# A two-layer transformer prompt kernel: three reciprocals of softmax sums moved to GpSimd as a power, the last tile's columns and store rearranged, and a new order list

## The chip, the cores and the metric

The kernel runs on one core of a Trainium2 chip. The core has five engines that run side by side, each with its own list of instructions: TensorE (PE, matmuls; PEld is its weight load), VectorE (DVE), ScalarE (ACT), GpSimd (POOL) and SyncE (SP, which only issues transfers). They wait for each other through semaphores. The metric is the device time of one execution in microseconds, as the median of several runs.

## What is computed

Two layers, each made twice with the same weights, on x of 2048 rows and 512 columns in bf16: attention over a sliding block of 256 keys with 32 heads of 16 columns, and an MLP of 1792 columns with gelu. Cut to what matters:

```python
def _A_ref(x, wqkv, wo):            # H = 32; Dh = 16; W = 256
    qkv = (x @ wqkv).reshape(B, S, 3, H, Dh)...
    scores = einsum("bhqd,bhkd->bhqk", q, k) * Dh ** -0.5
    mask = (i - j >= 0) & (i - j < W)
    p = softmax(where(mask, scores, -1e9))
    o = einsum("bhqk,bhkd->bhqd", p, v)
    return o.reshape(B, S, D) @ wo

def _B_ref(x, w1, b1, w2, b2):      # F = 1792
    return gelu(x @ w1 + b1) @ w2 + b2

x = x + _A_ref(layernorm(x)); x = x + _B_ref(layernorm(x))
x = x + _A_ref(layernorm(x)); x = x + _B_ref(layernorm(x))
```

## The kernel before

x lies in SBUF as 16 tiles of 128 rows; with the two repetitions there are 32 tile visits, called tau 0 to 31. Attention works on blocks b of two tiles (16 blocks), the MLP on jobs of two or four tiles.

For each block, Q, K and V are projected on TensorE into PSUM and copied out: Q and V by VectorE or ScalarE (line 725 or 727, whichever the list says), K by VectorE (line 853). The scores of a block are made in visits of 512 columns times four row groups, with small matmuls that run four at a time (`QT,KT`); ScalarE takes the exponential of each half visit (`E<-ps`, line 965), and VectorE or GpSimd multiplies the parts on the block's edge by a 0/1 mask (line 981).

P times V (`E,Va`) is made in pairs of 128-column groups, two pairs a block, so 32 in the whole kernel. V carries a column of ones, so each head's softmax sum comes out beside its 16 columns. Of each pair VectorE transposes the result out of PSUM into TT (line 1031); then the reciprocal of the sums is written into a spare column of TT, called Rc (line 1034, 32 numbers a partition); then TM = TT times Rc (line 1036, on VectorE or GpSimd); then VectorE transposes TM into OT (line 1041). There is one TT buffer and there are two TM buffers. When both pairs of a block are done, TensorE multiplies OT by `Wo_sb`, VectorE adds the result to x (line 793), and the layernorm for the MLP follows: statistics on VectorE (740, 742), the power -0.5 of the variance on GpSimd (744, one number a partition, with the constant tile `mhalf`), the scaling on VectorE or GpSimd (747), and a transposition by a trip through DRAM (two DMAs on SyncE's queue) or on TensorE. GpSimd adds b2 to x (1075).

The MLP multiplies by W1 (`xnTB,W_sb`), takes the gelu on ScalarE, either straight from PSUM (line 1111) or in wide pieces after VectorE has added b1 (lines 1100 and 1103), and multiplies by W2 (`W_sb,gT`). The exponential and the gelu need different tables on ScalarE; a change of table is a load of its own (ACT_TABLE_LOAD). The result is added to x (793), and in the second repetition each tile is stored from SyncE's queue as soon as it is done (1126). The very last tile, tau 31, is done in two column groups (1138, 1140), so that its addition and store can begin before its last matmul.

The program is recorded as some 3,200 nodes, each with an engine, what it reads and writes, and sometimes an alternative on another engine. Three tables of numbers, written out in the source, say the rest: `ORDER` the order in which the nodes are taken (each engine then runs its own in that order), `TURNS` which alternative each node with a choice takes, and `BANKS` which of the eight PSUM banks each group gets. The durations in the calls of `add` serve only to place waits within TensorE's stream; they do not change the order, which is given. GpSimd nodes that the source holds to be long (over 600 in any alternative) also wait for the VectorE operation marked `lock` that stands before them in the list.

Of the kernel before, what the change touches and what calls it, by code (L numbers as in the profile page):

```python
# [6 lines left out]
dt = mybir.dt  # L7
ALU = mybir.AluOpType
# [295 lines left out]
def bass_interleave_layers__sliding_block__dense_activation_gelu__prompt_kernel(  # L304
# [11 lines left out]
    Bb, S, D = A_x.shape  # L316
    assert Bb == 1
    P = 128
    T = S // P
    DC = D // P  # L320
    Dh = 16
# [63 lines left out]
    with ExitStack() as kctx:  # L385
        S_ = _Sched(nc, kctx)

        def sb(name, shape, dtype=dt.bfloat16):
            return kctx.enter_context(nc.sbuf_tensor(name, shape, dtype))
# [8 lines left out]
        statmv = sb("statmv", [P, NST, 2], dt.float32)  # L398
        mhalf = sb("mhalf", [P, 1], dt.float32)
# [15 lines left out]
        TT = sb("TT", [P, NTT, 2, 2, 8, 32], dt.float32)  # L415
        hot = TT[:, 0, 0, 0, 0, 0:HC]
        Rc = TT[:, :, :, :, :, VW]
# [211 lines left out]
        add = PL.add  # L629
# [5 lines left out]
            reads=["ident"], writes=["ident"])  # L635
# [573 lines left out]
```

## Time and profile before

| | us |
|---|---|
| median of 3 runs | 437.96 |
| lowest, highest | 437.73, 438.31 |
| the profiled execution | 437.65 |
| its span, first to last instruction | 435.8 |

The granted TensorE clock is 1.00 throughout. Some of the costliest groups (line, engine, operation, shapes, how many, then busy us and mean ns of one, then the idle time of the engine before them):

```profile
L965 ACT ACTIVATE E<-ps 128x1024 bf16<-128x1024 f32 x300 | 283.9, 1039 | 21.5 <-PE ps L32 20.0
L793 DVE TENSOR_TENSOR X<-X,ps 128x512 bf16<-128x512 bf16 x63 | 42.4, 679 | 25.7 <-PE ps L32 25.2
L1031 DVE STREAM_TRANSPOSE TT<-ps 128x1024 f32<-128x1024 f32 x32 | 39.9, 1247 | 11.8 <-PE ps L32 11.3
L740 DVE BATCH_NORM_STATS2 stat<-X 128x6 f32<-128x512 bf16 x64 | 42.6, 675 | 0.5 <-DMA X<-in_A_x_dram 0.2
```

How to read it: an engine's busy time says how much it has to do, and the idle time before a group says what it waited for. The chain of waits follows the work that ended last back to the start, at each step to whatever released it; time on that chain is time that the span consists of. Matmuls are pipelined, so one matmul's duration is longer than the step to the next one.

### The profile page before, as it was taken

Reading aid. Unit: us, or ns where it says so; the run is one execution under the profiler, and the core shown is the slowest. Engines: PE = TensorE matmul, PEld = TensorE weight load, DVE = VectorE, ACT = ScalarE, POOL = GpSimd, SP = SyncE. Lnnn points to the kernel's source line nnn. Section 1 sums busy time; section 2 is a strip of 40 time slices with the busy share of each in tenths; the row PEclk is TensorE's granted clock in tenths of the full one; section 3 lists DMA queues with packets and bytes.
Section 4 is the critical chain, followed back from the end, with each engine's and each line's share of the span. In section 5 each row is a group of like instructions: output and inputs, shape, how many; then the busy total and the mean of one; then the engine's idle time right before and its main releaser. Section 6 shows DMA issues by size and latency. Waiting matters only on the chain.

```text
span 435.8 us, 18376 instructions
## 1 busy us (share of the span) xinstructions
PE 419.3 (96%) x8281; PEld 251.6 (58%) x8338; DVE 367.3 (84%) x753; ACT 389.1 (89%) x452; POOL 272.4 (63%) x294
## 2 busy tenths in 40 slices
PE   8999999999799999999999999999999999999997
PEld 5767757665555546565555655644566554454674
DVE  6999999999999888999889788988989894766712
ACT  5999999999989999899898999799899999899551
POOL 6797949848755857858386556984535465576120
DMA  8930000001211023012211013000231003002201
GB/s 263 372 107 5 3 3 3 2 5 50 77 39 39 14 64 75 15 38 74 52 27 43 21 50 87 6 2 26 75 107 32 15 8 92 2 3 63 87 2 48
DMA packets 39898, 22.81 MB, mean 52 GB/s; under 512 B 24588, under 2 KB 39308, under 8 KB 39820
## 3 DMA queue, kind: packets, MB, share of 16 engines
q1 hardware_dynamic: 39404, 21.24, 16.7%
q8 instruction: 65, 1.06, 1.0%
q10 hardware_dynamic: 416, 0.39, 0.3%
q14 instruction: 13, 0.11, 0.1%
HBM read 13.77 MB, written 7.86 MB: 50 GB/s over the span
## 4 chain that ended last, share of the span: by engine, by line
PE 81%; ACT 14%; DVE 2%; issue 1%; DMA 1%; POOL 0%
PE ps L32 80%; ACT E L965 10%; ACT gT L1103 2%; ACT L1103 1%; PE ps L36 1%; ACT gT L1111 1%; ACT L965 1%; DMA X<-in_A_x_dram 1%; DVE stat L740 0%; DVE TT L1031 0%; DVE X L793 0%; DVE E L981 0%; DVE xn L747 0%; POOL statmv L744 0%; DVE X L1138 0%
## 5 line engine op out<-in xcount | busy, mean ns | idle before, releaser
L965 ACT ACTIVATE E<-ps 128x1024 bf16<-128x1024 f32 x300 | 283.9, 1039 | 21.5 <-PE ps L32 20.0
L981 POOL TENSOR_TENSOR E<-E,mask 128x512 bf16<-128x512 bf16 (+1 forms) x131 | 140.9, 1091 | 75.0 <-DVE E L981 39.7
L32 PE MATMUL ps<-xnTB,W_sb 128*128 128x512 bf16 (+1 forms) x560 | 117.3, 337 | 0.6 <-DVE E L981 0.2
L32 PE MATMUL ps<-W_sb,gT 128*128 128x512 bf16 (+2 forms) x419 | 107.7, 373 | 3.2 <-issue 2.4
L32 PE MATMUL ps<-xnTA,Wqkv_sb 128*128 128x256 bf16 (+1 forms) x544 | 74.2, 267 | 1.4 <-ACT E L965 1.1
L32 PEld LDWEIGHTS ps<-xnTB,W_sb 128*128 128x128 bf16 x560 | 51.8, 98 | 36.8 <-DVE TT L1031 0.2
L793 DVE TENSOR_TENSOR X<-X,ps 128x512 bf16<-128x512 bf16 x63 | 42.4, 679 | 25.7 <-PE ps L32 25.2
L32 PE MATMUL ps<-QT,KT 32*128 32x64 bf16 (+3 forms) x2392 | 60.6, 217 | 3.2 <-ACT E L965 1.2
L32 PEld LDWEIGHTS ps<-W_sb,gT 128*128 128x128 bf16 x462 | 40.1, 98 | 37.7 <-ACT gT L1111 0.5
L32 PEld LDWEIGHTS ps<-QT,KT 32*128 32x128 bf16 x2392 | 34.5, 92 | 46.9 <-ACT E L965 28.1
L32 PEld LDWEIGHTS ps<-xnTA,Wqkv_sb 128*128 128x128 bf16 x544 | 47.9, 98 | 17.4 <-ACT E L965 2.5
L981 DVE TENSOR_TENSOR E<-E,mask 128x512 bf16<-128x512 bf16 (+1 forms) x125 | 48.5, 415 | 9.8 <-ACT E L965 9.4
L1031 DVE STREAM_TRANSPOSE TT<-ps 128x1024 f32<-128x1024 f32 x32 | 39.9, 1247 | 11.8 <-PE ps L32 11.3
L1100 DVE TENSOR_SCALAR gT<-ps,b1T 128x512 bf16<-128x512 f32 (+1 forms) x72 | 45.0, 649 | 4.7 <-PE ps L32 4.2
L744 POOL TENSOR_TENSOR statmv<-statmv,mhalf 128x1 f32<-128x1 f32 x64 | 36.4, 577 | 18.7 <-DVE statmv L742 18.5
L32 PE MATMUL ps<-E,Va 64*17 64x64 bf16 (+3 forms) x3904 | 46.1, 229 | 2.0 <-PE ps L32 0.8
L1075 POOL TENSOR_TENSOR X<-X,b2b 128x512 bf16<-128x512 bf16 x32 | 36.9, 1154 | 16.9 <-DVE TM L1036 8.8
L1111 ACT ACTIVATE gT<-ps,b1T 128x512 bf16<-128x512 f32 (+1 forms) x68 | 36.0, 586 | 12.6 <-PE ps L32 12.4
L32 PEld LDWEIGHTS ps<-E,Va 64*17 64x17 bf16 x3904 | 36.8, 85 | 15.7 <-PE ps L32 5.1
L1036 POOL TENSOR_TENSOR TM<-TT 128x512 bf16<-128x512 f32 x24 | 26.6, 1107 | 27.0 <-DVE E L981 15.9
L853 DVE TENSOR_TENSOR KT<-ps,parmask 128x512 bf16<-128x512 f32 (+1 forms) x68 | 41.0, 644 | 2.4 <-PE ps L32 2.2
L740 DVE BATCH_NORM_STATS2 stat<-X 128x6 f32<-128x512 bf16 x64 | 42.6, 675 | 0.5 <-DMA X<-in_A_x_dram 0.2
(57 smaller groups left out, 380.3 us busy)
## 6 DMA issues: line engine op xcount, KB each, us to landing
scr_x<-xs_ SPq DMA_DIRECT2D x44, 128.0 KB, 1.8
W_sb<-in_B_w_dram SPq DMA_DIRECT2D x2, 1792.0 KB, 15.4
xnTB<-scr_x SPq DMA_DIRECT2D x26, 128.0 KB, 2.6
xnTA<-scr_x SPq DMA_DIRECT2D x18, 128.0 KB, 2.4
out_dram<-X SPq DMA_DIRECT2D x15, 128.0 KB, 1.9
Wqkv_sb<-in_A_wqkv_dram SPq DMA_DIRECT2D x4, 256.0 KB, 4.9
X<-in_A_x_dram SPq DMA_DIRECT2D x1, 1024.0 KB, 10.0
Wqkv_sb<-in_A_wqkv_dram SPq DMA_DIRECT2D x1, 512.0 KB, 6.3
```

Source lines behind the costliest of these rows:

```text
L32: return self.e.matmul(*a, **k)
L740: add("dve", lambda e, B: e.bn_stats(stat6[:, k6, 0:6], X[:, t, :]), 598, reads=["X%d" % t], writes=["st%d" % k6], prio=prio)
L744: add("pool", lambda e, B: e.tensor_tensor(out=statmv[:, m, 1:2], in0=statmv[:, m, 1:2], in1=mhalf[:], op=ALU.pow), 535, reads=["mv%d" % m ...
L793: add("dve", lambda e, B: e.tensor_tensor(out=X[:, t, :], in0=X[:, t, :], in1=ps[:, B[g][0], :], op=ALU.add), d_psum(512), reads=["X%d" % ...
L853: x = e.tensor_tensor(out=dst.rearrange("p (g s) (a k) -> p s g a k", s=2, a=2)[:, s], in0=src.rearrange("p (g s k) -> p s g k", s=2, k=HK ...
L965: add("act", lambda e, B, g_=g_, gi=gi: e.activation(E[:, 2 * gi : 2 * gi + 2, e0 : e0 + 512], ps[:, B[g_][0] : B[g_][0] + 2, :], AF.Exp, ...
L981: op = lambda e, B, Ew=Ew, Mw=Mw: e.tensor_tensor(out=Ew, in0=Ew, in1=Mw, op=ALU.mult)
L1031: add("dve", lambda e, B: e.transpose(TT[:, s].rearrange("p a c q d -> p a (c q d)"), ps[:, B[g][0] : B[g][0] + 2, :].rearrange("p a n -> ...
L1036: mul = lambda e, B: e.tensor_tensor(out=TM[:, sm].rearrange("p c q a d -> p a (c q) d"), in0=TT[:, s, :, :, :, 0:Dh].rearrange("p a c q d ...
L1075: add("pool", lambda e, B: e.tensor_tensor(out=X[:, t, :], in0=X[:, t, :], in1=b2b[:], op=ALU.add), 1110, reads=["X%d" % t, "b2b"], writes ...
L1100: add("dve", lambda e, B, g=g, fc=fc: e.tensor_scalar(out=gT[:, js % NG, fc, 0:M], in0=ps[:, B[g][0], 0:M], scalar1=b1T[:, fc : fc + 1], s ...
L1111: add("act", lambda e, B, g=g, fc=fc: e.activation(gT[:, js % NG, fc, 0:M], ps[:, B[g][0], 0:M], AF.Gelu_apprx_tanh, bias=b1T[:, fc : fc + ...
```

## The change

Four things change.

1. The reciprocal of the softmax sums gets an alternative on GpSimd: TT's sums to the power -1, with a constant tile of -1 (a second column of `mhalf`, filled by one more memset on GpSimd at the start). `TURNS` takes it for three of the 32 pairs: the sixth (block 2), the twenty-first (block 10) and the twenty-ninth (block 14). Since the alternative is booked at 1000, it is one of the nodes that wait for the VectorE operation before them.
2. In the last tile's two column groups the widths are exchanged between the groups, and the store of the group of 128 columns is issued from ScalarE's queue.
3. The booked duration of the reciprocal on VectorE goes from 264 to 300.
4. `ORDER`, `TURNS` and `BANKS` are new nearly throughout. Totals by engine: multiplications by Rc on VectorE 8, now 4 (GpSimd 24, now 28); scalings of the layernorm on VectorE 51, now 53 (GpSimd 13, now 11); Q copies on ScalarE 13, now 14 (VectorE 21, now 20); V copies on ScalarE 13, now 11 (VectorE 19, now 21); masks on VectorE 125, now 126 (GpSimd 131, now 130). TensorE's matmuls are the same.

```diff
-        mhalf = sb("mhalf", [P, 1], dt.float32)
+        mhalf = sb("mhalf", [P, 2], dt.float32)
...
         ORDER = [
-            20, 23, 4, 0, 21, 15, 5, 14, 1, 2, 6, 16, 7, 17, 18, 22, 3, 37, 38, 39, 43, 44, 40, 19, 45, 46, 85, 24, 41,
...
-        add("pool", lambda e, B: e.memset(mhalf[:], -0.5), 100, writes=["mhalf"])
+        add("pool", lambda e, B: e.memset(mhalf[:, 0:1], -0.5), 100, writes=["mhalf"])
+        add("pool", lambda e, B: e.memset(mhalf[:, 1:2], -1.0), 100, writes=["mone"])
...
-                out=statmv[:, m, 1:2], in0=statmv[:, m, 1:2], in1=mhalf[:], op=ALU.pow), 535,
+                out=statmv[:, m, 1:2], in0=statmv[:, m, 1:2], in1=mhalf[:, 0:1], op=ALU.pow), 535,
...
-                add("dve", lambda e, B: e.reciprocal(Rc[:, s], TT[:, s, :, :, :, Dh]), 264,
-                    reads=["TT%d" % s], writes=["Rc%d" % s], prio=pr - 800)
+                add("dve", lambda e, B: e.reciprocal(Rc[:, s], TT[:, s, :, :, :, Dh]), 300,
+                    reads=["TT%d" % s, "mone"], writes=["Rc%d" % s], prio=pr - 800,
+                    alt=(("pool", lambda e, B: e.tensor_tensor(out=Rc[:, s], in0=TT[:, s, :, :, :, Dh],
+                        in1=mhalf[:, 1:2, None, None].to_broadcast([P, 2, 2, 8]), op=ALU.pow), 1000),))
...
-                n = slice(0, 3 * P) if half == 0 else slice(3 * P, D)
+                n = slice(0, P) if half == 0 else slice(P, D)
...
-                    ["OUT%d_%d" % (t, half)], reads=["XL%d" % half], dur=1900.0, prio=prio)
+                    ["OUT%d_%d" % (t, half)], reads=["XL%d" % half], dur=1900.0, prio=prio, eng="sp" if half else "act")
```

Where the instructions stand now is seen best at three places.

The first is the end of TensorE's list: the product with W2 of tile 14 (512 columns) and of the last tile (its two column groups). Before, the group of 384 columns ends the list:

```order
L32 MATMUL ps<-W_sb,gT 128x384
L32 MATMUL ps<-W_sb,gT 128x128
L32 MATMUL ps<-W_sb,gT 128x384 x3
L32 MATMUL ps<-W_sb,gT 128x512 x2
L32 MATMUL ps<-W_sb,gT 128x384 x6
```

and now the group of 128 columns does:

```order
L32 MATMUL ps<-W_sb,gT 128x384 x2
L32 MATMUL ps<-W_sb,gT 128x128
L32 MATMUL ps<-W_sb,gT 128x384
L32 MATMUL ps<-W_sb,gT 128x512 x3
L32 MATMUL ps<-W_sb,gT 128x128 x11
```

So the wide group is finished first, then tile 14, and eleven narrow matmuls are last; in both lists the addition and the store of tile 14 stand just before those of the last group.

The second is ScalarE's list at the first MLP job: exponentials, a change of table, gelus in wide pieces (`gT<-gT`) and straight from PSUM (`gT<-ps,b1T`), and a change back. Before:

```order
L965 ACTIVATE E<-ps 128x2x512 x8
L1103 ACT_TABLE_LOAD
L1103 ACTIVATE gT<-gT 128x4x256 x2
L727 ACTIVATE Va<-ps 128x2x16x16
L1111 ACTIVATE gT<-ps,b1T 128x256 x2
L1103 ACTIVATE gT<-gT 128x4x256
L965 ACT_TABLE_LOAD
```

and now:

```order
L966 ACTIVATE E<-ps 128x2x512 x8
L1106 ACT_TABLE_LOAD
L1106 ACTIVATE gT<-gT 128x4x256
L1114 ACTIVATE gT<-ps,b1T 128x256
L1106 ACTIVATE gT<-gT 128x4x256
L1114 ACTIVATE gT<-ps,b1T 128x256
L1106 ACTIVATE gT<-gT 128x4x256
L966 ACT_TABLE_LOAD
```

The copy of V has left the block; VectorE makes that copy now.

The third is VectorE's list at the sixth pair, whose reciprocal is the first to move. Before:

```order
L1031 STREAM_TRANSPOSE TT<-ps 128x1024
L725 CAST Va<-ps 128x2x16x16
L1034 RECIPROCAL TT<-TT 128x32
L853 TENSOR_TENSOR KT<-ps,parmask 128x4x128 x2
L725 CAST QT<-ps 128x2x256
L1041 STREAM_TRANSPOSE OT<-TM 128x512
```

and now, on VectorE and, in the second fence, on GpSimd:

```order
L1032 STREAM_TRANSPOSE TT<-ps 128x1024
L726 CAST Va<-ps 128x2x16x16
L854 TENSOR_TENSOR KT<-ps,parmask 128x4x128 x2
L726 CAST QT<-ps 128x2x256
L1044 STREAM_TRANSPOSE OT<-TM 128x512
```

```order
L982 TENSOR_TENSOR E<-E,mask 128x4x128
L745 TENSOR_TENSOR statmv<-statmv,mhalf 128x1
L1037 TENSOR_TENSOR TT<-TT,mhalf 128x32
L1039 TENSOR_TENSOR TM<-TT 128x2x16x16
```

The reciprocal has gone from between the two copies; on GpSimd the power stands right ahead of the multiplication that uses it, so no other engine lies between the two.

391 rows, old and new, of tables (BANKS, ORDER, TURNS) are left out of this document.

## The prediction

> **What bounds the kernel now.** I read the page first: the busy totals, then the shares of the chain that ended last.
>
> ```profile
> span 435.8 us, 18376 instructions
> PE 419.3 (96%) x8281; PEld 251.6 (58%) x8338; DVE 367.3 (84%) x753; ACT 389.1 (89%) x452; POOL 272.4 (63%) x294
> PE 81%; ACT 14%; DVE 2%; issue 1%; DMA 1%; POOL 0%
> ```
>
> TensorE holds the chain for 81% of the span and ScalarE for 14%; VectorE and GpSimd hold almost none of it. So work taken from VectorE pays only where VectorE decides when TensorE or ScalarE goes on. The shares are averages, so I cut the middle of the span into stretches (length, then busy us of PE, PEld, DVE, ACT, POOL):
>
> ```profile
> 20.00:60.00 40.00, 38.77 (x823) 27.66 (x827) 37.97 (x86) 39.06 (x46) 32.34 (x36) 1.00 0.15 47
> 60.00:100.00 40.00, 38.66 (x1000) 26.12 (x1005) 38.38 (x85) 38.62 (x43) 27.95 (x29) 1.00 0.02 7
> 100.00:140.00 40.00, 36.17 (x926) 21.02 (x917) 38.08 (x74) 38.72 (x43) 28.04 (x29) 1.00 0.20 52
> 340.00:433.00 93.00, 91.06 (x1385) 51.23 (x1396) 57.71 (x106) 73.24 (x95) 40.41 (x39) 1.00 0.12 35
> ```
>
> From 20 to 140 us three engines are full at once: VectorE idles 5.57 us of 120 (2.03 + 1.62 + 1.92), ScalarE 3.60, TensorE 6.40. In the last 93 us VectorE idles 35 us while TensorE idles 1.9: there VectorE work is free. Next I read the chain in order of time inside the full stretch:
>
> ```profile
> 44.59 1.94 ACT E L965 x2
> 46.55 1.28 ACT L1103
> ...
> 49.84 0.51 ACT Va L727
> ...
> 52.03 1.28 ACT L965
> ...
> 98.70 18.45 ACT E L965 x20
> ```
>
> From 44.6 to 55 us the chain runs through ScalarE: a table load, the gelus of the first MLP job, one copy of V, the table load back. From 98.7 to 117.1 it is nothing but exponentials. The 3.83 us that TensorE idles in 100 to 140 therefore lie mostly under ScalarE's exponentials, and a better TensorE order alone does not win them back.
>
> **The change part by part.** The sum starts at the profiled execution, 437.65 us (435.8 of span and 1.85 around it), which is 0.31 under the median of 437.96; I add the difference to the median.
>
> The end first. Here TensorE has run out of other work:
>
> ```profile
> 428.40 4.34 PE L32 MATMUL ps<-W_sb,gT 128*128 128x512 bf16 x27
> 430.88 0.29 DVE L1138 TENSOR_TENSOR X<-X,ps 128x128 bf16<-128x128 bf16 x1 [1.16 <-PE ps L32]
> 431.80 0.69 DVE L793 TENSOR_TENSOR X<-X,ps 128x512 bf16<-128x512 bf16 x1 [0.63 <-PE ps L32]
> 432.77 0.56 DVE L1138 TENSOR_TENSOR X<-X,ps 128x384 bf16<-128x384 bf16 x1 [0.28 <-PE ps L32]
> ...
> out_dram<-X SPq DMA_DIRECT2D x1, 96.0 KB, 1.6
> out_dram<-X SPq DMA_DIRECT2D x1, 32.0 KB, 1.4
> X<-in_A_x_dram SPq DMA_DIRECT2D x1, 128.0 KB, 2.4
> X<-in_A_x_dram ACTq DMA_DIRECT2D x1, 128.0 KB, 2.7
> ```
>
> Behind the last matmul stand an addition of 0.56 us and the 96 KB store (the last four rows are KB and us to landing). With 128 columns last they become 0.29 us and 32 KB: 0.27 and 0.2 us less. Against that stands tile 14's own addition of 0.69 us, which starts when its last 512-column matmul ends. The 27 matmuls in 4.34 us hold 9,856 columns (8 of 512, 13 of 384, 6 of 128 by the order before), 0.44 ns a column, so the eleven of 128 columns that now follow it last about 0.62 us, and the last addition waits 0.07 us for VectorE. That makes -0.40. ScalarE's queue is otherwise idle by then; the only pair of equal loads shows 2.7 us on it against 2.4 on SyncE's, at the crowded start, so at worst +0.3. I take **-0.35**, with ends -0.4 and -0.1.
>
> The row of the 32 KB store bears on a page. The Trainium skill (DMA: Bandwidth & Descriptors, Specifications) asks for at least 512 B per transfer, with read-modify-write below; 128 bf16 columns are 256 B a row, so by that rule the store's gain would be lost and the end would give -0.15. The rows, 1.4 us at 256 B a row and 1.6 at 768 B, disagree, and I keep them.
>
> The second term is the V copy in ScalarE's chain. The new order leaves it out of the first gelu block and VectorE makes it: the form rows are
>
> ```profile
> L727 ACT ACTIVATE Va<-ps 128x512 bf16<-128x512 f32 x13 | 8.3, 638 | 0.0
> L725 DVE CAST Va<-ps 128x512 bf16<-128x512 f32 x19 | 12.7, 675 | 1.0 <-PE ps L32 0.9
> L747 DVE TENSOR_SCALAR xn<-X,statmv 128x512 bf16<-128x512 bf16 x51 | 21.0, 424 | 1.6 <-POOL statmv L744 1.6
> L1034 DVE RECIPROCAL TT<-TT 128x32 f32<-128x32 f32 x32 | 11.0, 343 | 0.4
> L1036 DVE TENSOR_TENSOR TM<-TT 128x512 bf16<-128x512 f32 x8 | 5.5, 683 | 0.1
> L981 DVE TENSOR_TENSOR E<-E,mask 128x512 bf16<-128x512 bf16 x110 | 44.8, 434 | 9.8 <-ACT E L965 9.4
> L981 DVE TENSOR_TENSOR E<-E,mask 128x256 bf16<-128x256 bf16 x15 | 3.6, 274 | 0.0
> L744 POOL TENSOR_TENSOR statmv<-statmv,mhalf 128x1 f32<-128x1 f32 x64 | 36.4, 577 | 18.7 <-DVE statmv L742 18.5
> L1036 POOL TENSOR_TENSOR TM<-TT 128x512 bf16<-128x512 f32 x24 | 26.6, 1107 | 27.0 <-DVE E L981 15.9 <-DVE TT L1034 5.7 <-DVE xn L747 5.4
> L747 POOL TENSOR_SCALAR xn<-X,statmv 128x512 bf16<-128x512 bf16 x13 | 27.0, 2080 | 6.3 <-DVE TM L1036 2.7 <-DVE xn L747 1.8 <-DVE E L981 1.7
> ```
>
> On the chain the copy held 0.51 us. I take **-0.5**; the low end is its full 0.64, the other end 0, if VectorE, which takes 0.675 us more in a full stretch, becomes late by as much.
>
> The third is the three powers on GpSimd: VectorE loses 3 x 0.343 = 1.03 us. No row shows a power of 32 numbers a partition. The nearest, on the same engine with the same operation, is the power of one number, 577 ns: that is the low end. If each further number cost as much again, it would be 32 x 0.577 = 18.5 us: the high end. I take 1 us, close to the nearest row, and ask what each place can hide. The first (sixth transposition) in the trace before:
>
> ```profile
> 78.06 0.34 DVE L1034 RECIPROCAL TT<-TT 128x32 f32<-128x32 f32 x1
> 78.47 1.11 POOL L1036 TENSOR_TENSOR TM<-TT 128x512 bf16<-128x512 f32 x1 [0.40 <-DVE TT L1034]
> 80.05 0.70 DVE L1041 STREAM_TRANSPOSE OT<-TM 128x512 bf16<-128x512 bf16 x1
> 81.94 0.59 PE L32 MATMUL ps<-Wo_sb,OT 128*128 128x512 bf16 x2
> ```
>
> The transposition ended at 77.55 and the reciprocal queued behind a V copy, so a power of about 0.9 us started at 77.55 would leave the multiplication where it is. Behind it, 0.47 us lie between the multiplication's end and the next transposition, and 1.19 between that one's end (80.75) and the output projection: **0** up to a power of about 2.5 us, and no gain either, since TensorE did not wait there. The other two have more room. At 258.79 the multiplication followed 1.9 us after the reciprocal's start, at 367.42 it followed 10.7 us after:
>
> ```profile
> 258.79 0.35 DVE L1034 RECIPROCAL TT<-TT 128x32 f32<-128x32 f32 x1
> 260.71 1.11 POOL L1036 TENSOR_TENSOR TM<-TT 128x512 bf16<-128x512 f32 x1 [2.80 <-DVE xn L747]
> 367.42 0.35 DVE L1034 RECIPROCAL TT<-TT 128x32 f32<-128x32 f32 x1
> 378.15 0.69 DVE L1036 TENSOR_TENSOR TM<-TT 128x512 bf16<-128x512 f32 x1
> ```
>
> The third power has a new waiter: the new order puts the multiplication on VectorE soon after it, with a residual and a mask behind. That is in the stretch where VectorE has room, so 0 again.
>
> The fourth is the rest of the order. Of the other VectorE work, four multiplications go to GpSimd (-2.73 us), two scalings come back (+0.85), and copies and masks add about 1.1: VectorE is 1.8 us lighter in all. GpSimd gains 4 x 1.107, loses 2 x 2.08 and one mask, and makes three powers: 2 to 3 us more, of 163 idle. But up to the sixth transposition (76.31 us before) VectorE's rows hold one V copy (0.675) and three masks (0.434 and two of 0.274) more and one statistic (0.675) less, about +1.0 us, and up to the sixteenth still +0.6. I take **0** for it, because 5.57 us idle stand against it, and keep +1.0 as an end. TensorE changes the kind of matmul 369 times instead of 367; a change out of a score group shows as
>
> ```profile
> 359.53 1.24 PE L32 MATMUL ps<-W_sb,gT 128*128 128x512 bf16 x5 [0.16 <-issue]
> ```
>
> so two of them cost at most 0.32 and perhaps nothing: **+0.2**. The table loads are 20 in both.
>
> **Sum:** -0.35 - 0.5 + 0 + 0 + 0.2 = -0.65, 437.0 us for an execution like the profiled one and **437.3** on the median. Its own range goes from 436.7 (the low ends) to 438.2 (the high ends without the VectorE term).
>
> **The rivals.** *The new list fills waits that the old one left.* TensorE idles 435.8 - 419.3 = 16.5 us; the end takes 3.1, the start 1.2 and the window under the exponentials 3.8, so 8.4 are left in small waits. For it: nearly every stretch is re-dealt. Against it: in both lists ScalarE runs the same 52 exponentials without a break after the second gelu block, and the load on each engine per block hardly differs. A quarter filled gives 437.3 - 2.1 = 435.2.
>
> *VectorE becomes late in the first third.* Place: 20 to 140 us, where the order has up to 1.0 us more ahead of its transpositions and copies for TensorE. It decides once the extra work falls where VectorE had no idle time; then the V copy's 0.5 is not won and 1.0 is paid, and what is late there pushes ScalarE's chain, so it is not made up: 437.96 - 0.35 + 0.2 + 1.0 = 438.8, and 439.8 if a second wait of that size follows, say 439.3. For it, TensorE already waits for a VectorE copy there:
>
> ```profile
> 114.12 0.40 PE L32 MATMUL ps<-QT,KT 32*128 32x128 bf16 x16 [1.05 <-DVE KT L853]
> ```
>
> Against it: that wait lies under the 18.45 us of exponentials, and VectorE's share of the chain is 2%.
>
> *The power is long.* From 2.5 us on, the first place pays what is beyond: at 6 us it is 3.5, so 440.8. The high end, 18.5, would give 453. Against it: a power on its own takes 577 ns, most of which a second number need not pay again. A page leans the other way too: the Trainium skill (GPSIMD Engine Reference, Performance versus the Vector engine) puts GpSimd's elementwise work at about 2.6 cycles an element against VectorE's 1; no run here shows that figure for a power.
>
> **How the numbers follow.** The sum 0.42, waits filled 0.28, VectorE late 0.20, a long power 0.08, another loss 0.02. 0.2%, about what a measurement can tell, is 0.88 us: faster means below 437.08, slower above 438.84. Of the sum's 0.42 I give 0.15 to faster and 0.27 to the middle; waits filled is all faster; VectorE late, the power and the rest are slower. So faster 0.43, same 0.27, slower 0.30. The range, 434.8 to 439.9, reaches over the second and third case and leaves out the long power and a larger gain, some 0.17.
>
> **What would show it.** The end: the last addition 0.29 us long, starting within 0.4 us of the last matmul's end, and the last store landing in about 1.4 us. The V copy: no Va row in the chain between the first two table loads, and the exponential behind them 0.5 us earlier. The powers: three POOL rows, about 1 us each, with no wait of PE or DVE on them above 0.5 us. The order: PE's idle time in 140 to 433 within a microsecond of before. A power above 2.5 us, or DVE entries in the chain between 60 and 120 us, would make the prediction wrong on the slow side; a PE busy share that rises by half a percent, on the fast side.

## The result, and the profile after

The changed kernel takes **451.06 us** (median of 4 runs, 450.47 to 451.33) against 438.13 beside it: a ratio of 1.0295, 95% interval [1.0282, 1.0308]. It is slower by 13 us; 437.3 was predicted, with a range up to 439.9. The likeliest case was wrong, and so was the range. Of the small gains that were forecast some can be seen in the trace and none in the time; what decides is the price of the three powers.

The page of the changed kernel, in four rows: the span, the busy totals, TensorE's granted clock in 40 slices, and the shares of the chain that ended last.

```profile
span 449.6 us, 18449 instructions
PE 432.4 (96%) x8338; PEld 253.6 (56%) x8338; DVE 366.4 (82%) x750; ACT 388.5 (86%) x451; POOL 286.6 (64%) x299
PEclk9999999799999999999999999999999999799999
PE 80%; ACT 8%; DVE 6%; POOL 3%; issue 1%; DMA 1%; POOLq 0%
```

VectorE is 0.9 us less busy than before (367.3), ScalarE 0.6 less: the work itself hardly changed. TensorE's busy total can't be set against the 419.3 of before, where 57 of its records are missing; the same list without the powers (an experiment below) has 426.0 for the same 8338 matmuls, so here they take 6.4 us more. A busy time that grows with equal work is no wait: it is the same work done more slowly, and the clock row has two dips, where the kernel before kept 1.00 throughout. GpSimd is 14 us busier, and it now has 3% of the chain. The next view is the powers' own line: its durations, and who waited for it.

```profile
L1037 POOL TENSOR_TENSOR TT<-TT,mhalf x3: 5469/5469/5469, 78.0 to 375.7; 128x32 f32<-128x32 f32 x3
...
who waited for it (us, times):
  DVE TM L1039: 5.6, 1
```

A power of 32 numbers a partition takes **5.47 us**, each time alike; 1 us had gone into the sum. This view names one waiter only, because in the other two places the next one is on GpSimd itself. To see what a place costs, the order of time has to be read. The first place (start, length, engine and line, and in brackets the idle time ahead with what ended it):

```profile
77.96 5.47 POOL L1037 TENSOR_TENSOR TT<-TT,mhalf 128x32 f32<-128x32 f32 x1
...
81.38 0.72 PE L32 MATMUL ps<-Wqkv_sb,xnTA 128*128 128x256 bf16 x5
83.51 1.10 POOL L1039 TENSOR_TENSOR TM<-TT 128x512 bf16<-128x512 f32 x1
...
84.64 0.71 DVE L1044 STREAM_TRANSPOSE OT<-TM 128x512 bf16<-128x512 bf16 x1 [4.24 <-POOL TM L1039]
85.28 1.25 DVE L854 TENSOR_TENSOR KT<-ps,parmask 128x512 bf16<-128x512 f32 x2
85.41 0.39 PE L32 MATMUL ps<-Wqkv_sb,xnTA 128*128 128x256 bf16 x1 [3.31 <-DVE OT L1044]
85.60 1.48 PE L32 MATMUL ps<-Wo_sb,OT 128*128 128x512 bf16 x3
```

The power, the multiplication, VectorE's transposition and TensorE's output projection follow each other without a gap. VectorE stands 4.24 us with the K and V copies behind its transposition; TensorE stands 3.31 us. Its first three output-projection matmuls then take 1.48 us, 0.49 each: slow ones. The same stretch cut into pieces of 2 us (length, busy us of PE, PEld, DVE, ACT, POOL, then the granted clock):

```profile
82.00:84.00 2.00, 0.10 (x1) 0.00 (x0) 0.00 (x0) 1.46 (x2) 1.92 (x2) 1.00 0.03 8
84.00:86.00 2.00, 0.59 (x2) 0.28 (x3) 1.36 (x3) 0.00 (x0) 1.72 (x2) 0.69 0.00 0
86.00:88.00 2.00, 2.00 (x21) 0.61 (x20) 1.76 (x4) 0.32 (x1) 0.16 (x1) 0.50 0.00 0
88.00:90.00 2.00, 2.00 (x7) 0.72 (x5) 0.78 (x2) 1.62 (x2) 2.00 (x3) 0.50 0.00 0
90.00:92.00 2.00, 2.00 (x30) 1.44 (x29) 1.40 (x3) 1.10 (x2) 1.72 (x2) 0.60 0.00 0
92.00:94.00 2.00, 2.00 (x27) 1.09 (x26) 1.98 (x6) 1.59 (x2) 1.08 (x1) 1.00 0.00 0
```

TensorE stands still, and when its work comes back the clock is at 0.50 for some 6 us: full again only from 92 us. So the place is paid for twice, once as a standstill and once as slow work. The Trainium skill (TensorE: Matmul & The Clock Gate, The HAM clock gate) has this rule: after about 3.4 us of idling TensorE is clocked at half, and it is back at full speed after about as long of steady work. The trace has the halving and the return, at other lengths. Standstills of 3.31 us here and of 2.96 at the third place were enough, and the mean of 0.69 in the piece from 84 us, between 1.00 and 0.50, puts the fall at about 84.8, some 2.7 us after TensorE's last matmul had ended (82.10). The return came some 6 us after the work did.

At the third place the wait goes another way:

```profile
375.69 5.47 POOL L1037 TENSOR_TENSOR TT<-TT,mhalf 128x32 f32<-128x32 f32 x1 [0.23 <-DVE TT L1032]
...
381.19 0.69 DVE L1039 TENSOR_TENSOR TM<-TT 128x512 bf16<-128x512 f32 x1 [5.58 <-POOL TT L1037]
381.80 0.68 DVE L794 TENSOR_TENSOR X<-X,ps 128x512 bf16<-128x512 bf16 x1
...
382.63 0.61 PE L32 MATMUL ps<-QT,KT 32*128 32x64 bf16 x16 [2.96 <-DVE X L794]
```

VectorE waits 5.58 us for the power with a residual behind it. The residual empties a PSUM bank, and the next scores need that bank. TensorE has nothing to do with the pair whose sums are being turned; it stands because VectorE is blocked in order.

I compare two executions by when the same exponential of the 300 on ScalarE starts; they are numbered from 0 to 299. Against the changed kernel with its three reciprocals put back on VectorE (the second experiment below), the changed one is level at the 54th exponential (-0.03 us), 6.18 late at the 72nd, 5.98 at the 204th, 7.67 at the 222nd, 7.66 at the 276th and 13.43 at the 288th and the last. So the three places take **6.2, 1.7 and 5.8 us**, and what lies between them takes nothing (0.2 us come back).

### The profile page after: what moved, and what is told of

It is laid out like the page before. It is cut to its first block, busy times and chain, and to the rows that moved or that the text cites. A ratio compares the mean times of both kernels' runs of the same rounds, so it can differ in the third digit from the quotient of the medians.

```text
span 449.6 us, 18449 instructions
## 1 busy us (share of the span) xinstructions
PE 432.4 (96%) x8338; PEld 253.6 (56%) x8338; DVE 366.4 (82%) x750; ACT 388.5 (86%) x451; POOL 286.6 (64%) x299
## 3 DMA queue, kind: packets, MB, share of 16 engines
q8 instruction: 65, 1.06, 1.1%
## 4 chain that ended last, share of the span: by engine, by line
PE 80%; ACT 8%; DVE 6%; POOL 3%; issue 1%; DMA 1%; POOLq 0%
PE ps L32 79%; ACT E L966 7%; POOL TT L1037 2%; PE ps L36 1%; DVE E L982 1%; DVE stat L741 1%; DVE KT L854 1%; POOL E L982 1%; DVE X L794 1%; ACT gT L1106 1%; DMA X<-in_A_x_dram 1%; DVE TT L1032 1%; POOL TM L1039 0%; DVE QT L726 0%; DVE xs_ L758 0%
## 5 line engine op out<-in xcount | busy, mean ns | idle before, releaser
L32 PE MATMUL ps<-xnTB,W_sb 128*128 128x512 bf16 (+1 forms) x560 | 119.3, 342 | 0.0
L32 PE MATMUL ps<-W_sb,gT 128*128 128x512 bf16 (+2 forms) x462 | 119.2, 374 | 0.0
L32 PE MATMUL ps<-xnTA,Wqkv_sb 128*128 128x256 bf16 (+1 forms) x544 | 75.9, 268 | 1.6 <-DVE X L794 0.8
L32 PEld LDWEIGHTS ps<-xnTA,Wqkv_sb 128*128 128x128 bf16 x544 | 48.2, 98 | 18.5 <-ACT E L966 2.1
L745 POOL TENSOR_TENSOR statmv<-statmv,mhalf 128x1 f32<-128x1 f32 x64 | 35.5, 562 | 26.8 <-DVE statmv L743 26.8
L1039 POOL TENSOR_TENSOR TM<-TT 128x512 bf16<-128x512 f32 x28 | 31.0, 1106 | 22.3 <-DVE E L982 13.8
```

What stands on the lines that cost most here:

```text
L32: return self.e.matmul(*a, **k)
L745: add("pool", lambda e, B: e.tensor_tensor(out=statmv[:, m, 1:2], in0=statmv[:, m, 1:2], in1=mhalf[:, 0:1], op=ALU.pow), 535, reads=["mv%d ...
L1039: mul = lambda e, B: e.tensor_tensor(out=TM[:, sm].rearrange("p c q a d -> p a (c q) d"), in0=TT[:, s, :, :, :, 0:Dh].rearrange("p a c q d ...
```

## The experiments

**The price of the power by itself.** Powers of growing width at the end of GpSimd's list, where it has nothing else to do:

```diff
+        for n in (1, 2, 4, 8, 16, 32):
+            add("pool", lambda e, B, n=n: e.tensor_tensor(
+                out=pw[:, 0, 0:n], in0=pw[:, 0, 0:n], in1=mhalf[:, 0:1].to_broadcast([P, n]), op=ALU.pow), 535,
...
+        add("pool", lambda e, B: e.tensor_tensor(
+            out=pw[:, 1], in0=pw[:, 0], in1=pw[:, 1], op=ALU.mult), 100, reads=["pw"], writes=["pw"])
```

> The kernel before with powers of 1, 2, 4, 8, 16 and 32 numbers a partition and one multiplication of 32 put at the end of GpSimd's list, on a tile of their own, in stretches where GpSimd has nothing else. By a line through 0.577 us (1 number) and 5.469 us (32): 0.58, 0.73, 1.05, 1.68, 2.94 and 5.47 us, 0.158 us a number. If the 5.47 us come instead from the strided operands of the sums, a power over adjacent numbers is much shorter, nearer 1 us. Time as before, 437.5 to 438.5 us.

The groups by line and shape (busy us, mean ns of one):

```profile
L1159 POOL TENSOR_TENSOR pw<-pw,mhalf 128x32 f32<-128x32 f32 x1 | 5.4, 5414 | 0.1
L1159 POOL TENSOR_TENSOR pw<-pw,mhalf 128x16 f32<-128x16 f32 x1 | 2.9, 2895 | 0.1
...
L1159 POOL TENSOR_TENSOR pw<-pw,mhalf 128x2 f32<-128x2 f32 x1 | 0.7, 702 | 0.1
L1159 POOL TENSOR_TENSOR pw<-pw,mhalf 128x1 f32<-128x1 f32 x1 | 0.6, 556 | 0.1
L1162 POOL TENSOR_TENSOR pw<-pw 128x32 f32<-128x32 f32 x1 | 0.3, 251 | 0.1
```

Nearly a straight line: 556 ns for one number and (5414 - 556)/31 = **157 ns** for each further one, on adjacent numbers as on the strided sums. A multiplication of the same 32 numbers takes 251 ns in all, so it is the power and not the engine that is dear. The time, 437.78 us in one run, is that of the kernel before.

**The new order without the powers.** The three reciprocals go back to VectorE; all else is the changed kernel.

```diff
+        for k in (114, 349, 465):
+            TURNS[k] = 0
```

> The changed kernel with its three powers made as reciprocals on VectorE again, all else as changed. If the three powers (5.47 us each in the trace) and what follows from them are the whole loss, the exponentials' starts say that 6.2 + 1.4 to 1.9 + 6.2 us go away: 436.8 to 437.8 us, granted clock 1.00 throughout, i.e. the new order is worth 0.3 to 1 us by itself. Rival: the new order is slower by itself and the powers only part of it: 441 to 449. Second rival: the drop of the clock comes from the denser order and not from the standstills, then it stays and the time is 443 to 445.

438.02 us (437.38 to 441.78 in 10 runs; ratio 1.0012, [0.9993, 1.0032]), just above what was expected. All 13 us are the powers', and the rest of the change is worth nothing that can be measured.

**The powers alone, in the old order.**

```diff
...
+                if (b, cp) in ((2, 1), (10, 0), (14, 0)):
+                    add("pool", lambda e, B: e.tensor_tensor(out=Rc[:, s], in0=TT[:, s, :, :, :, Dh],
+                        in1=mhalf[:, 1:2, None, None].to_broadcast([P, 2, 2, 8]), op=ALU.pow), 1000,
+                        reads=["TT%d" % s, "mhalf"], writes=["Rc%d" % s], prio=pr - 800)
...
```

> The kernel before, its order untouched, with the same three reciprocals as powers on GpSimd. If the power is the cause, the first place costs some 6 us (its slack there is about 1.7 us against 4.5 us more), the second 1 to 2, the third less than in the changed kernel, since its multiplication stands 10 us behind the reciprocal: 444 to 449 us, with a drop of the clock in the stretch from 80 to 95. Rival (the order is the cause): 437.5 to 440.

452.48 us (ratio 1.0323, [1.0306, 1.0341]): as dear as in the new order and above the 444 to 449 expected, because the places share the loss otherwise. By the exponentials the first costs 5.7 us, the second 8.5 (1 to 2 had been expected) and the third 0.3. The second, in order of time:

```profile
264.73 5.47 POOL L1039 TENSOR_TENSOR TT<-TT,mhalf 128x32 f32<-128x32 f32 x1 [5.57 <-DVE TT L1035]
270.14 0.55 POOL L748 TENSOR_TENSOR statmv<-statmv,mhalf 128x1 f32<-128x1 f32 x1
...
270.72 1.23 DVE L751 TENSOR_SCALAR xn<-X,statmv 128x512 bf16<-128x512 bf16 x1 [6.07 <-POOL statmv L748]
...
272.20 0.68 DVE L797 TENSOR_TENSOR X<-X,ps 128x512 bf16<-128x512 bf16 x1
...
272.94 0.61 PE L32 MATMUL ps<-QT,KT 32*128 32x128 bf16 x16 [5.97 <-DVE X L797]
```

Neither VectorE nor TensorE waits for the power's result here. A layernorm's small power is queued behind it on GpSimd, VectorE's scaling waits 6.07 us for that, a residual stands behind the scaling, and TensorE waits 5.97 for the residual's bank. Which place is dear depends on what the list has put behind the long instruction.

**One power at a time, in the new order**: two of the three turns set back each time.

> The changed kernel with the first power alone (sixth pair), the other two on VectorE. If the places add up independently: without powers about 437.3, plus 6.2: 443 to 444, one drop of the clock, at 84 to 92 us. Rival (a power only sets off what the order would lose anyway): under 440.

> The new order with one of its three powers alone, that of the 21st pair (the second place); the other two reciprocals are on VectorE again. If the loss at a place is made by TensorE's standstill and the half clock behind it, this place is the cheap one: in the changed kernel TensorE never stood longer than about 0.8 us here, so no clock below 0.99, and 438.0 (the new order with no power) + 1.4 to 1.9 = 439.4 to 439.9 us. If each power costs about the same through its length alone, a third of 13 us: 442.4 us.

> The changed kernel with the third power alone (twenty-ninth pair). If the places add up: 437.3 + 6.2 = 443 to 444, one drop of the clock, shortly after 375 us. Rival: in the stretch where VectorE idles a third of the time its wait is made up and the time is under 440.

| power kept | time, us | ratio [95%] | over 438.02 |
|---|---|---|---|
| first place | 443.58 | 1.0122 [1.0107, 1.0138] | 5.6 |
| second | 440.08 | 1.0051 [1.0030, 1.0071] | 2.1 |
| third | 443.84 | 1.0124 [1.0098, 1.0149] | 5.8 |

Each place costs by itself; none needs another. Together they make 13.4 us and the three at once 13.0, but that the two agree so well is in part luck. By the exponentials the places alone cost 5.8, 1.7 and 4.6 us, 12.1 in all. The profiled executions with the second and with the third power lose another 0.4 and 0.9 us to a dip of the clock between 115 and 120 us, far ahead of their power. The second is the cheap one: its 1.7 us is what was expected, and the dip lifts the time 0.2 us above its range. TensorE stands only 0.82 us there, and a third of 13 us, the rival's 442.4, is well off:

```profile
259.90 5.46 POOL L1039 TENSOR_TENSOR TT<-TT,mhalf 128x32 f32<-128x32 f32 x1
...
270.00 0.28 PE L32 MATMUL ps<-xnTA,Wqkv_sb 128*128 128x256 bf16 x1 [0.82 <-DVE X L796]
```

**Powers of half the length.**

```diff
-                    alt=(("pool", lambda e, B: e.tensor_tensor(out=Rc[:, s], in0=TT[:, s, :, :, :, Dh],
-                        in1=mhalf[:, 1:2, None, None].to_broadcast([P, 2, 2, 8]), op=ALU.pow), 1000),))
+                    alt=(("pool", lambda e, B: e.tensor_tensor(out=Rc[:, s, 0:1], in0=TT[:, s, 0:1, :, :, Dh],
+                        in1=mhalf[:, 1:2, None, None].to_broadcast([P, 1, 2, 8]), op=ALU.pow), 1000),))
```

> The changed kernel, but each of its three powers makes 16 of the 32 numbers a partition; the other 16 reciprocals are left out. By 0.577 us for one number and 5.469 us for 32, a power takes 2.9 to 3.0 us here, so each standstill is 2.5 us shorter: 0.8 us at the first place, 0.4 at the third, none at the second, too short for the clock to fall. Theory (standstill plus half clock): clock 1.0 and 438.0 + 1.2 = 439.2 us (438.8 to 440). Rival (loss in proportion to the power's length): 438.0 + 13 x 2.95/5.47 = 445 us.

440.04 us (ratio 1.0060, [1.0036, 1.0083]), just above the first theory's range and far from the rival's 445. The first place:

```profile
78.06 2.93 POOL L1037 TENSOR_TENSOR TT<-TT,mhalf 128x16 f32<-128x16 f32 x1
...
82.20 0.71 DVE L1044 STREAM_TRANSPOSE OT<-TM 128x512 bf16<-128x512 bf16 x1 [1.70 <-POOL TM L1039]
...
82.97 0.28 PE L32 MATMUL ps<-Wqkv_sb,xnTA 128*128 128x256 bf16 x1 [0.77 <-DVE OT L1044]
```

A standstill of 0.77 us, where 0.8 was expected, and a clock of 1.0 throughout. By the exponentials the places cost 1.6, 0 and 0.5 us, at the first twice its standstill. Taking 46% off the length takes 85% off the loss (2.0 us instead of 13.0 over 438.02).

**The waits filled.** This should split a place into standstill and half clock: TensorE works through most of its wait on matmuls that nobody reads, ahead of the waiting node, into an idle bank.

```diff
+        KEEP = {526: (2, 13), 2746: (4, 12)}
...
+            if i in KEEP:
+                S_.op("pe", lambda e, bk=KEEP[i][0], m=KEEP[i][1]: [e.matmul(ps[:, bk, :], W1_sb[:, 0, 0:P],
+                      W1_sb[:, 1, 0:512], start=True, stop=True) for _ in range(m)][-1],
+                      reads=["W1"], writes=["bank%d" % KEEP[i][0]], start=-1e9, n=KEEP[i][1])
```

> The changed kernel with 13 and 12 added matmuls of 512 columns on TensorE, into an idle bank, just ahead of the matmul that waits at the first and at the third place; nobody reads what they make. The waits are as long as before (about 3.3 and 3.0 us of no useful work), but TensorE is busy in them. Theory: the half clock that follows is gone (0.99 or more in those stretches) and each place costs 2.3 to 2.9 us less: 451.1 - 5.2 = 445.9 us (445.2 to 447). Rival (the clock only witnesses the delay, the queue behind the wait is what costs): 450.5 to 451.5 us.

The total missed: 451.56 us (ratio 1.0315, [1.0295, 1.0335]), the rival's number to 0.1 us. The clock did what the theory said, though, 1.00 behind both waits, and the places were cheaper. By the exponentials, in us later than the kernel without powers (profiled executions):

| at exponential | changed | filled (bf16) | filled (fp32) | short matmuls, no power |
|---|---|---|---|---|
| 54 | -0.03 | -0.16 | 0.68 | 0.06 |
| 72 | 6.18 | 3.75 | 4.57 | 0.43 |
| 96 | 6.06 | 6.90 | 7.16 | 3.63 |
| 276 | 7.66 | 9.54 | 9.25 | 4.33 |
| 288 | 13.43 | 12.58 | 12.29 | 4.68 |
| 299 | 13.43 | 13.47 | 12.29 | 5.26 |

At the first place the filled wait costs 3.9 us instead of 6.2 and at the third 3.0 instead of 5.8; but between the 72nd and the 96th exponential another 3.2 us go, where the changed kernel loses nothing. So the first theory did not hold as it stood, and I formed another for that stretch: the added instructions move something on TensorE. Two runs test it, a control with as many, but short, matmuls and no power, and a filling with few instructions:

The control has the three turns set to 0 as above and, in the added matmuls,

```diff
+        KEEP = {526: (2, 13), 2746: (4, 12)}
...
+                S_.op("pe", lambda e, bk=bk, m=m: [e.matmul(ps[:, bk, 0:64], W1_sb[:, 0, 0:P],
+                      W1_sb[:, 1, 0:64], start=True, stop=True) for _ in range(m)][-1],
+                      reads=["W1"], writes=["bank%d" % bk], start=-1e9, n=m)
```

and the filling is the changed kernel with

```diff
+        KEEP = {526: (2, 3), 2746: (4, 3)}
...
+                S_.op("pe", lambda e, bk=bk, m=m: [e.matmul(ps[:, bk, :], W1_sb[:, 0, 0:2 * P].bitcast(dt.float32),
+                      W1_sb[:, 1, 0:1024].bitcast(dt.float32), start=True, stop=True) for _ in range(m)][-1],
+                      reads=["W1"], writes=["bank%d" % bk], start=-1e9, n=m)
```

> The new order with no power (438.0 us) and, at the two places where the last kernel had 13 and 12 matmuls of 512 columns, as many of 64 columns, which nobody reads. They fill no wait; by the shortest groups of matmuls here they take some 0.06 us each, 0.8 and 0.7 us. Theory: in the run with the long ones the gain at the first place was lost again because 26 more instructions moved TensorE's pauses that end with 'issue' (0.61 to 0.82 us at 105, 117 and 122 us): then the same pauses come here, a loss of 2 to 3 us between the 72nd and the 96th exponential, and 441.5 to 443 us. Rival (it was lost to something in the wait itself): 439.0 to 439.8 us, no such pauses.

> The changed kernel with 3 and 3 added matmuls of 512 columns in fp32 ahead of the two waiting matmuls instead of 13 and 12 in bf16; nobody reads what they make. If one takes four times a bf16 one (0.22 us), TensorE is busy for 2.6 us of each wait with 6 added instructions rather than 26. Theory: no half clock behind the two waits, 2.4 and 2.7 us less at them (as in the run with bf16 matmuls), and with the instructions hardly moved it is kept: 451.1 - 5.1 = 446 us (445 to 447.5). Rival (what the clock gives back is lost in the next stretch anyway, to the other engines): 450.5 to 451.5 us.

The control: 443.09 us (ratio 1.0112, [1.0094, 1.0130]), just above what was expected. Matmuls that cost 0.4 us at the first place cost 5 us in all, 3.2 of them in that same stretch (last column). So what the filled runs lost there is lost without a power too. Its pauses:

```profile
101.70 0.31 PE L32 MATMUL ps<-QT,KT 32*128 32x192 bf16 x7 [0.61 <-issue]
113.10 0.38 PE L32 MATMUL ps<-QT,KT 32*128 32x64 bf16 x13 [0.59 <-issue]
...
118.97 1.20 PE L32 MATMUL ps<-E,Va 64*17 64x128 bf16 x62 [0.29 <-issue]
```

They end with "issue", that is, with nothing that the profile shows, and break a group of sixteen score matmuls into 3 and 13. The filled run has them too (0.64, 0.61 and 0.82 us at 105, 117 and 122 us); the changed kernel has one of 0.52, the kernel without powers one of 0.51. The fp32 filling, which the chip ran as six matmuls at each place, came to 449.77 us (ratio 1.0257, [1.0240, 1.0274]): a miss against 446. It kept what it won at the third place to the end (column fp32: 9.25 to 12.29, then nothing more), and lost 2.6 us in the same stretch as the others, with pauses of 0.57 and 0.54. Six added matmuls were not few enough. The pauses are not all: in that stretch the clock of all three goes to half, from 123 to 126 us in the bf16 filling, from 119 to 126 in the fp32 one and from 116 to 123 in the control.

**Each place filled alone.** The third has no such stretch behind it. It has the third power alone, and the fp32 matmuls there:

```diff
+        KEEP = {2746: (4, 3)}
```

The other has the first power alone, and 128 bf16 matmuls of 32 columns, which were to add one whole packet of instructions:

```diff
+        KEEP = {526: (2, 128)}
```

> The new order with the power of the third place alone (443.84 us before) and 3 fp32 matmuls of 512 columns, which nobody reads, ahead of the matmul that waits there. In the run with both places filled this place cost 3.04 us instead of 5.77 and nothing was lost behind it. Theory (the half clock after the standstill is worth 2.7 us here): no clock below 0.99 around 380 to 392 us and 443.8 - 2.7 = 441.1 us (440.6 to 441.7). Rival (the next stretch takes it back): 443 to 444.5 us.

> The new order with the power of the first place alone (443.58 us before) and 128 short matmuls (32 columns) ahead of the matmul that waits there, which nobody reads. The profile of the changed kernel shows 65 instruction packets of 1.06 MB for some 16.7 thousand instructions of TensorE and its weight loads: 256 instructions a packet. 128 matmuls with their loads are one packet, so the pauses behind the place should fall where they fell without them. At 0.03 us each they take some 3.7 us, 0.4 more than the wait. Theory (half clock worth 2.4 us here; what the other filled runs lost again came from moved pauses): 443.6 - 2.4 + 0.4 = 441.6 us (441 to 442.3), no pauses over 0.5 us between 95 and 125 us but that at about 123. Rival (VectorE and ScalarE take the gain back): 443.3 to 445 us.

Third place: 440.82 us (ratio 1.0071, [1.0048, 1.0094]) where 441.1 was expected and 443.84 stood without the filling. The wait, filled:

```profile
371.60 2.74 PE L32 MATMUL ps<-W_sb 128*128 128x512 f32 x6
373.30 0.69 DVE L1041 TENSOR_TENSOR TM<-TT 128x512 bf16<-128x512 f32 x1 [5.59 <-POOL TT L1039]
374.73 0.41 PE L32 MATMUL ps<-QT,KT 32*128 32x64 bf16 x16 [0.39 <-DVE X L796]
```

VectorE waits 5.59 us as ever, the clock stays at 1.00, and the sixteen score matmuls take 0.41 us, where they took 0.62 behind the empty wait. By the exponentials the place costs 3.0 us with the filling and 4.6 without; most of what is left of the 3.0 us between the two medians is the dip of the clock between 116 and 120 us that the profiled execution without the filling had (0.9 us). In the changed kernel, where the clock stayed at half for 6.8 us instead of 3.4, the place costs 5.8. So the half clock is worth 1.5 us in the one and 2.7 in the other.

First place: 443.22 us (441.44 to 443.34), no better than 443.58 and a miss. The clock stays full and the place costs 3.9 us, as in both other filled runs, instead of 5.8 (this power alone) or 6.2, but pauses of 0.41 and 1.06 us at 102 and 122 us come back. A whole packet did not keep them away. What the half clock costs at the first place, 1.9 us (this power alone) or 2.3 (changed kernel), is shown at the place alone, not by a total time.

**Two parts of the rest.** The memset of Va's ones back to GpSimd's start, in the new order without powers; and the moved V copy alone, in the old order.

```diff
+        ORDER.remove(15)
+        ORDER.insert(ORDER.index(0) + 1, 15)
```

```diff
+        TURNS[89] = 0
```

> The new order with no power, and GpSimd's memset of Va's ones back near the start of its list (0.91 us, beside nothing that VectorE does yet). The first exponential was 0.87 us later in the changed kernel than before, with that memset beside VectorE's scaling of xn, which took 1.17 us against 0.41. If that overlap is the cause, the first exponential is 0.5 to 0.9 us earlier, and the time 437.2 to 437.6 us where the lead is kept to the end; 438.0 if it is the order of other work that makes the late start.

> The kernel before with one copy alone moved: the V copy on ScalarE ahead of the first gelu block goes to VectorE, as in the change. By the two traces the change gained 0.36 us between the 30th and the 36th exponential: 437.98 - 0.36 = 437.6 us, if the rest of the order keeps it; 438.0 if VectorE, late there, gives it back.

The memset: 438.06 us, ratio 0.9999 [0.9988, 1.0010]. The cause of the slow scaling is shown: in the changed kernel the two ran beside each other,

```profile
5.78 1.17 DVE L748 TENSOR_SCALAR xn<-X,statmv 128x512 bf16<-128x512 bf16 x1 [0.31 <-POOL statmv L745]
5.89 0.91 POOL L669 MEMSET Va<- 128x192 bf16 x1
```

and with the memset at 1.11 us the scaling is back at 0.41:

```profile
1.11 0.91 POOL L673 MEMSET Va<- 128x192 bf16 x1
...
5.87 0.41 DVE L752 TENSOR_SCALAR xn<-X,statmv 128x512 bf16<-128x512 bf16 x1 [0.31 <-POOL statmv L749]
```

But the first exponential came only 0.28 us earlier, and no gain shows in the time. The V copy alone: 438.13 us, ratio 0.9999 [0.9989, 1.0008]. It won 0.13 us between the 30th and the 36th exponential and had given it back by the 42nd. Neither makes a kernel that beats the one before.

## Why the prediction was wrong, step by step

**The step that failed** is in the third term: "I take 1 us, close to the nearest row". The term was mis-sized: 5.47 us. The two bounds, 0.577 and 18.5, held it, but the value was taken at the low end, on the ground that a second number need not pay again "most of" what one power takes. The row of one number could not tell a fixed cost from a cost per number, and the width run shows that 157 of its 556 ns are paid again each time.

**The slack was read at one waiter.** "**0** up to a power of about 2.5 us" at the first place was close: 5.47 - 2.5 gives 3.0 us, and TensorE stood 3.31. At the second, 1.9 us had been read as slack; 3.8 us of the power were hidden and 1.7 paid, and half the length cost nothing. At the third, "that is in the stretch where VectorE has room, so 0 again" is wrong in kind. An engine that idles 35 of 93 us has room for more work, but it runs its list in order; whatever stands behind a waiting instruction waits as well. The prediction named the new waiter and the residual behind it, and did not ask who waits for that residual.

**What was in no term** is the clock. A standstill of 3 us brought some 6 us at half speed, 2.3 us more at the first place and 2.7 at the third. So the rival of the long power, "at 6 us it is 3.5, so 440.8", had the mechanism and a chance of 0.08, and a price a quarter of the real one: it counted one place of three, and at that place the standstill alone. With 3.9 + 1.7 + 3.0 for the waits and 2.3 + 2.7 for the clock the sum is 13.6 us. These are the three places' costs again, split by the filled runs, so that they meet the 13.5 between the two profiled spans is no test of the split; the medians differ by 13.0.

**The end**, -0.35: the last addition took 0.29 us and started 0.04 us after the last matmul's end, as put. But the store, on ScalarE's queue, took 1.7 us where the same size took 1.4 on SyncE's:

```profile
446.77 0.29 DVE L1141 TENSOR_TENSOR X<-X,ps 128x128 bf16<-128x128 bf16 x1
...
out_dram<-X ACTq DMA_DIRECT2D x1, 32.0 KB, 1.7
```

From the last matmul's end to the span's it is 2.87 us against 3.06: -0.19, between the two ends given. It is read from the traces; this part was not run by itself.

**The V copy**, -0.5: the exponential behind the first gelu block gained 0.36 us on the kernel before, of the 0.51 that the copy had held. Alone in the old order it gained 0.13, and not for long. Right in direction, and not kept.

**The rest of the order**, 0 and +0.2: the list without powers takes 438.02 us, so the gains of these two steps are eaten. In part this is the start, which nobody had costed: the first exponential came 0.87 us later than before, beside the moved memset. The low end of the sum's own range, 436.7, is a slip of 0.2: its terms give 437.96 - 0.4 - 0.64 = 436.9. It changes nothing here.

"Waits filled" (435.2) had a premise that the trace did not bear. Its 16.5 us of idle TensorE, 8.4 of them in small waits, come from a trace with 57 matmuls fewer than weight loads, and a missing record reads as idle time. The old order with one copy moved (the V copy run) has them all:

```profile
PE 426.0 (98%) x8338; PEld 251.4 (58%) x8338; DVE 367.9 (84%) x754; ACT 388.7 (89%) x451; POOL 272.2 (62%) x294
```

That leaves 9.9 us idle, and from 140 to 433 us, where the trace of before shows 5.4, this one shows 0.4. There was next to nothing to fill there. Neither this rival nor "VectorE late" (439.3) came about: from the 96th to the 276th exponential the list without powers is at no point more than 0.1 us ahead of the kernel before or 1.0 behind it.

## What to carry to other kernels

Where the trace has an operation at one size only, no value inside the bounds is the cautious one: work out the time at both bounds, and let the sum go by the dear one unless a second size rules it out. Ask of a long instruction on a side engine what stands behind it in that engine's list and behind its waiter in the waiter's list, and follow that to TensorE; room on the waiter's engine does not help. A standstill of TensorE near 3 us is paid for again in slow matmuls, so a wait cut below a microsecond is worth more than its length. And compare the numbers of matmuls and of weight loads in a trace before TensorE's idle time is read from it.

## What the runs showed of the hardware

The clock can also fall without a standstill. In the control with short matmuls and no power, TensorE never stood longer than 1.01 us between 109 and 118 us, but it was busy for 1.11 and 0.97 of 2 us in two pieces on end, and the clock then went to half for 6.8 us:

```profile
112.00:114.00 2.00, 1.11 (x22) 0.78 (x22) 1.97 (x3) 1.63 (x3) 1.74 (x2) 1.00 0.37 131
114.00:116.00 2.00, 0.97 (x21) 0.40 (x18) 1.24 (x4) 2.00 (x3) 0.39 (x1) 1.00 0.54 123
116.00:118.00 2.00, 1.56 (x80) 1.28 (x80) 2.00 (x5) 2.00 (x3) 1.60 (x2) 0.53 0.36 80
```

A low busy share does not bring the fall each time. The kernel without powers goes through the same work with pieces of 0.87, 1.48, 1.02 and 1.35 us and keeps 1.00, and its least busy 3.4 us there hold 1.6 us of work, as in the control. Nor are added instructions needed: the runs with the second and with the third power alone have their dip in this stretch too, and four of the ten executions of the kernel without powers have a mean clock of 0.992. With the short matmuls added all four have it. So this stretch lies near an edge in all these kernels; that, with the pauses, is where the filled runs lost what they had won. Every dip in the middle of these traces, behind a standstill or not, lasts 3.4 or 6.8 us. What sets off a dip here, and what decides where the pauses fall, stays open.
